# Attention and an MLP on one core: the first-layer products of half of d_ff as seven block products for eight

## The chip, the cores and the metric

The kernel runs on one core of a Trainium2 chip. The metric is the device time of one execution in microseconds, lower is better. The core has five engines with a queue each, which work in order and wait for one another by semaphores: TensorE (PE in the profile, its weight loads PEld), VectorE (DVE), ScalarE (ACT), GpSimd (POOL) and SyncE (SP), which issues most DMAs. TensorE's results go to PSUM, eight banks of 512 fp32 values for each of 128 partitions; the other data lie in SBUF.

## The reference

```python
q_n = q / (norm(q) + 1e-6);  k_n = k / (norm(k) + 1e-6)      # (8, 12, 448, 64) each
attn = softmax(q_n @ k_n.T / tau)                            # tau 0.1
x = (attn @ v).transpose(0, 2, 1, 3).reshape(3584, 768)
h = x @ w_in                                                 # 768 x 2048
g = h * clip(h + 3, 0, 6) / 6
out = g @ w_out                                              # 2048 x 768, fp32
```

## The kernel before

The eight batches of 448 tokens are worked on by pairs of heads, 48 pairs in all, six to a batch. A start-up written out by hand (`PLAN`) takes pairs 0 to 17. Then the loop of L999 runs one **turn** for each pair i from 18 to 47, some 7.8 us long, and after it a list `units[NP]` ends the work. Everything is issued in the order of the program text; no planner moves anything, so what an engine does next is what stands next in its queue.

A turn computes scores of its pair (seven 448-column matmuls in four groups, the last one, "M", apart), their exponentials on ACT (`exps`, L440), the products with v of the pair before (`values`, L462), and on DVE the division by the row sums (`finish_values`, L482 and L483: one reciprocal a pair, by which turns are found in the trace). Between them it runs **units** of the MLP, out of the list `units[i]`:

- `mm1_unit` (L561) is one of the 16 blocks of 128 columns of d_ff of one batch: six matmuls of 448 columns into one PSUM bank (L567), a relu on ACT (L576) and a product on DVE (L582) into g. Batch b's blocks run in turns 6(b+1) to 6(b+1)+5, and two are carried to the next batch's first turn.
- `product_unit` (L721) is one of the seven block products with which two blocks of 128 tokens of the second layer are computed already: eight matmuls of 384 columns (L740). It draws on sums of g that DVE makes (`g_sum`, L718), which stand in the dictionary `side` and are issued in a turn just behind `finish_values`.
- `single_unit` (L811) and `mm2_unit` (L607) are the second layer's other products.

Behind each unit `whole_units` (L940) issues its work on ACT and on DVE. In a turn the order is: scores of three groups, their six exponentials, values, `finish_values`, the sums of `side`, the first unit, the scores M and their exponential, the other units with the odd turns' norms and copies between them, the row sums of squares of a later pair (`reduce`, L238), loads of later q, k and v (`LQ`, `LV`, on SP), and the first group of values.

PSUM banks of scores and units come out of one ring of six (`next_bank`, L163); a bank is written again when its readers are done. Raw q and k lie in seven buffers (five from pair 26 on), their squares in two, values in three, all parts of the tile `big`, whose unused end also holds g of the last batch and late sums (`tail`, L531). The probabilities (`at`) go round six buffers.

Of the kernel before, what the change touches and what calls it, by code (L numbers as in the profile page):

```python
# [61 lines left out]
def kernel(  # L62
# [43 lines left out]
    gs = {x: const.tile([128, KC, 128], BF16, name=f"gs{x}", tag=f"gs{x}") for x in ("1", "6", "70", "71")}  # L106
    KM = 3 * 128
    kz = [const.tile([128, 4 * 128], BF16, name=f"kz{i}", tag=f"kz{i}") for i in range(2)]
    km = const.tile([128, 2, 128], BF16, name="km", tag="km")
# [25 lines left out]
    def raw_before(j):  # L135

        return j - NR if j < 26 else j - NR + 2

    def raw_buffer(j):
        return raws[j % NR if j < 26 else (j - 26) % (NR - 2)]  # L140

# [15 lines left out]
    ring_n = [0]  # L157

    def next_bank():
        ring_n[0] += 1  # L160
        return ring[(ring_n[0] - 1) % len(ring)]

    raw_of, sq_of, nrm_of, at_of, on_of = {}, {}, {}, {}, {}  # L163
# [37 lines left out]
    def load_v(d):  # L201
        needs(("VC", 2 * (d - NV)), ("VC", 2 * (d - NV) + 1))
        b, n = 2 * d // HP, 2 * d % HP
        for g in range(2):
            f = v[b, HP * g + n : HP * g + n + 2].rearrange("i (p c) d -> p i (c d)", c=7)
            t = vr[d % NV][:, 2 * g : 2 * g + 2, :, :].rearrange("p i c d -> p i (c d)")
            for half in range(2):
                o = t[64 * half : 64 * half + 64, :, (1 - half) * D : (5 - half) * D]
                nc.sync.dma_start(out=o, in_=f[:, :, 3 * half * D : (3 * half + 4) * D])

    def square(j, e, c0, n):

        heads = range(c0 // 7, (c0 + n - 1) // 7 + 1) if j < 2 else (0, 1)
        needs(("RE", j - 2), *(("LQ", j, g) for g in heads))
        if j not in sq_of:
            sq_of[j] = sqs[j % 2], []
        sq, have = sq_of[j]
        have.extend(range(c0, c0 + n))
        if j < 2:
            o, i = (x[:, :, :, :].rearrange("p g c d -> p (g c) d")[:, c0 : c0 + n, :] for x in (sq, raw_of[j]))  # L220
        else:
            o, i = sq[:, :, c0 : c0 + n, :], raw_of[j][:, :, c0 : c0 + n, :]
        if e == "a":
            nc.scalar.activation(out=o, in_=i, func=AF.Square)  # L224
        else:
            engines[e].tensor_tensor(out=o, in0=i, in1=i, op=ALU.mult)  # L226
# [58 lines left out]
    def vcast(i, e):  # L285
        needs(("LV", i // 2), ("VA", i - NVX, 3))
        t = vr[i // 2 % NV][:, i % 2, 1:5, :]
        f = bass.AP(tensor=t.tensor, offset=t.offset, ap=[t.ap[0], [9 * D, 2], [D, 4], [1, D]])
        o = vx[i % NVX][:, :, 0:D].rearrange("p (g c) d -> p g c d", g=2)
        if e == "v":  # L290
            nc.vector.tensor_reduce(out=o, in_=f.rearrange("p g c (d x) -> p g c d x", x=1), axis=AX.X, op=ALU.max)
            return
        (engines[e].copy if e == "a" else engines[e].tensor_copy)(out=o, in_=f)  # L293
# [101 lines left out]
    def scores(i, g, bank=None):  # L395
# [9 lines left out]
        for n, name in enumerate(GROUPS[g]):  # L405
            if name == "M":
                rows, c0 = slice(0, 128), KM
            else:
                rows = slice(64 * n, 64 * n + 64)
                c0 = 128 * int(name[1])  # L410
            if bank is None:
                o, key = bank_of(None, 1)
                keys.append(key)
                o = o[:, 0:S]
            else:
                o = SC[bank][:, n, 0:S]
            if name == "M" and i < HP:
                for rows in (slice(0, 64), slice(64, 128)):
                    nc.tensor.matmul(o[rows, :], kt[rows, KM : KM + SR], qt[rows, :], start=True, stop=True)
            else:  # L420
                ks = km[:, i % 2, :] if name == "M" and i >= XJ else kt[rows, c0 : c0 + 128]
                nc.tensor.matmul(o, ks, qt[rows], start=True, stop=True)  # L422
            out.append(o)
        sc_of[(i, g)] = (out if bank is None else [SC[bank][:, 0 : len(GROUPS[g]), 0:S]]), keys
        if g == 3:
            issued.add(("SM", i))

    def exps(i, g):
        m = len(GROUPS[g])
        at = ats[m][at_n[m] % len(ats[m])]  # L430
        at_n[m] += 1
# [98 lines left out]

    def tail(c, n):  # L531

        assert 2 * RAW <= c and c + n <= (NR + 2) * RAW + NV * VAL
        return big[:, c : c + n]

    TAIL = 2 * RAW
    g_last = tail(TAIL, FCN * (S + SR) // 2).bitcast(BF16).rearrange("p (f n) -> p f n", f=FCN)
    TAIL += FCN * (S + SR) // 2

# [21 lines left out]
    def mm1_unit(b, fc):  # L561
        needs(*(("CX", i) for i in range(b * HP, (b + 1) * HP)))
        assert len(weights) <= 6 - 2 * (2 * fc // FCN)
        x, g, c0 = xT[b % 2], g_of(b), b % 2 * SR
        ps, key = bank_of(None, 1)
        for cc in range(CC):
            nc.tensor.matmul(  # L567
# [13 lines left out]
        def product(u):  # L581
# [8 lines left out]
            unread[key] = 0  # L590
            g_done.add((b, fc))

        post["a"].append(relu)
# [44 lines left out]
    def second(b):  # L638
# [12 lines left out]
    banks, parts, ready = {}, {}, set()  # L651
    late_sums = [
        {x: tail(c, SUM).bitcast(BF16).rearrange("p (c n) -> p c n", c=KC) for x, c in zip("167e", range(c, c + 4 * SUM, SUM))}
        for c in (TAIL, TAIL + 3 * SUM)
    ]
    late_sums[0].pop("e")
    TAIL += 7 * SUM
    wide = [big[:, c : c + MH] for c in range(0, 3 * MH, MH)]
    wide_late = [tail(c, MH) for c in range(TAIL, TAIL + 2 * (len(PAIRS) - LOOP) * MH, MH)]

# [59 lines left out]

    def product_unit(n, name, end=None, apart=False):  # L721

# [4 lines left out]
        base = None if apart else {"2": "4", "5": "3", "6": "1"}.get(name)  # L727
        if base is None:
            banks[n, name] = bank_of(None, 1)
        ps, key = banks.pop((n, base)) if base else banks[n, name]  # L730
        c0, width = (MH // 2 * end, MH // 2) if end in (0, 1) else (0, MH)
# [6 lines left out]
        m = ps[:, c0 : c0 + width]  # L738
        for c in range(KC):
            nc.tensor.matmul(  # L740
# [5 lines left out]
                skip_group_check=True,  # L746
            )
        issued_products.add((n, name))
        d, e = d_and_e(n)
# [61 lines left out]
    def single_unit(b, m):  # L811

        t = 2 + b % 2
        assert all((x, c) in summed for x in ("y3", "y4") for c in range(KC)) and (b, "e") in g_summed
        ps, key = bank_of(None, 1)
        w = w_out_sb[:, :, m * MH : m * MH + MH].rearrange("p (c k) m -> p c k m", k=2)
        for n in range(2):
# [24 lines left out]
    def products(text):  # L842
# [26 lines left out]
        43: sums(6, "75"), 44: sums(6, "62"), 45: sums(6, "1"), 46: sums(7, "75"), 47: sums(7, "62"),  # L869
    }  # L870
    units = {}
    carry = firsts(1, FCN - 2, FCN - 1)
    for b in range(2, B - 1):
        first = firsts(b, *range(FCN))
        for n, x in enumerate([0, 3, 3, 3, 3, 2]):
            i = (b + 1) * HP + n
            u = carry + [first.pop(0) for _ in range(x)]
            carry = []
            *p, last = products(TURNS[i])
            if i == NP - 1:  # L880
                p, last = [last], None
# [6 lines left out]
    b = B - 1  # L888
    f = firsts(b, *range(FCN))
    units[NP] = sums(7, "1") + carry[:1] + products("4.7") + carry[1:] + [(g_left, B - 2)] + products("2.7")  # L890
    units[NP] += products("3.8") + sums(8, "75") + products("1.7 4.8") + sums(8, "62") + products("6.7 5.8") + sums(8, "1")
    units[NP] += products("7.7") + sums(B - 2, "e")
    for n, x in enumerate("2176"):
        units[NP] += f[n : n + 1] + products(x + ".8")
    units[NP] += f[4:] + products(f"s{B - 2}.0") + sums(9, "75") + products(f"s{B - 2}.1") + sums(9, "62")
    units[NP] += products("3.9 4.9") + sums(9, "1") + products("5.9") + sums(10, "75") + products("2.9 3.10") + sums(10, "62")
# [43 lines left out]
    def whole_units(n, engines="av"):  # L940
        for _ in range(n):
            unit()
            for e in engines:
                while post[e]:
                    finish_units(e)

    OPS = {
# [48 lines left out]

    if FIRST + 6 < NP:
        do("LQ", FIRST + 6)
    for i in range(FIRST, NP):  # L999
# [39 lines left out]
        if not even:  # L1039
            prepare(("NO", (i + 3) // 2))  # L1040
            if n_u > 3 and stream[0][0] is product_unit and units[i][1][0] is mm1_unit:
                do("UU", 1)
                n += 1
            prepare(("CK", i + 1), ("CK", i + 2))
# [4 lines left out]
        do("UU", 1)  # L1049
        prepare(("RE", i + 5), ("LQ", i + 7))  # L1050
        if not even:
            prepare(("LV", (i + 5) // 2))
        while post["p"]:
# [44 lines left out]
```

## Time and profile before

| what | value |
|---|---|
| runs | 405.30, 405.31, 406.76 us; median 405.31 us |
| profiled execution | 404.91 us, its span 403.1 us |
| granted TensorE clock | 1.000 |
| DVE busy | 286.4 us, 71% of the span, 503 instructions |
| ACT busy | 278.3 us, 69% |
| POOL busy | 234.0 us, 58% |
| first-layer matmuls (L567) | 768 of 448 columns |
| second-layer block products (L740) | 624 matmuls, 608 of them of 384 columns, 16 of 192 |

A span runs from the first to the last instruction; the rest of an execution's time lies around it. A matmul's duration on the page runs to a modelled end and overlaps the next one, so the rate at which TensorE works is read from the starts of matmuls that follow one another: the chain of waits lists them so.

### The profile page before, as it was taken

To read this page: it belongs to the slowest core of one execution; us is meant where nothing else is said; L and a number is where in the kernel's file an instruction comes from. 1 tells how busy PE (TensorE), PEld (TensorE's weight loads), DVE (VectorE), ACT (ScalarE), POOL (GpSimd) and SP (SyncE) were. 2 spreads that over 40 slices of the span, in tenths; PEclk is the share of its full clock that TensorE was granted. 3 is DMA by queue.
4 is the path that set the end of the run, shared out by engine and by line. 5 is a ranking of instruction groups with operands and counts; after the bars stand their busy time and mean duration, and the time that the engine had idled before them with its cause. 6 is when DMAs were issued, how large, how long until landed. Compare 5 with 4: busy or idle time off the path is not lost.

```text
span 403.1 us, 9619 instructions
## 1 busy us (share of the span) xinstructions
PE 395.5 (98%) x3696; PEld 234.3 (58%) x3696; DVE 286.4 (71%) x503; ACT 278.3 (69%) x609; POOL 234.0 (58%) x228
## 2 busy tenths in 40 slices
PE   7999999999999999999999999999999999999996
PEld 4666656555655556556555556555565556555563
DVE  5898768766998777776867888687656566644663
ACT  5999998798467686786858768668658755225230
POOL 7799655662384997488386865766665500510070
PEclk9999999999999999999999999999999999999999
DMA  8999989979988659786989659976963523130134
GB/s 289 281 254 257 216 247 230 156 125 230 187 213 220 139 128 228 171 222 130 180 216 212 152 130 164 182 192 145 192 154 76 112 46 67 41 79 21 26 73 99
DMA packets 91566, 65.32 MB, mean 162 GB/s; under 512 B 56064, under 2 KB 89984, under 8 KB 91520
## 3 DMA queue, kind: packets, MB, share of 16 engines
q1 hardware_dynamic: 87408, 58.02, 62.8%
q0 software_dynamic: 3712, 6.29, 9.0%
q8 instruction: 29, 0.48, 0.5%
q10 hardware_dynamic: 400, 0.39, 0.3%
q14 instruction: 17, 0.14, 0.1%
HBM read 47.19 MB, written 11.01 MB: 144 GB/s over the span
## 4 chain that ended last, share of the span: by engine, by line
PE 94%; DVE 3%; DMA 1%; ACT 0%; issue 0%; DVEq 0%; ACTq 0%
PE M L567 24%; PE M L740 17%; PE PV L462 13%; PE Y L567 6%; PE M L422 6%; PE Z L567 5%; PE Y L740 4%; PE Z L740 4%; PE M L614 3%; PE M L820 2%; PE Z L422 2%; PE PV L922 2%; PE Z L820 1%; PE Y L422 1%; DVE n L238 1%; PE SC L422 1%
## 5 line engine op out<-in xcount | busy, mean ns | idle before, releaser
L440 ACT ACTIVATE at<-M 128x448 bf16<-128x448 f32 x200 | 99.9, 568 | 16.4 <-PE M L422 14.4
L567 PE MATMUL M<-xT,w_in_sb 128*128 128x448 bf16 x522 | 110.8, 352 | 0.0
L567 PEld LDWEIGHTS <-w_in_sb 128*128 128x128 bf16 x768 | 72.0, 98 | 62.6 <-issue 2.8
L274 POOL TENSOR_TENSOR nrm<-big,r 128x896 bf16<-128x896 f32 (+1 forms) x48 | 79.5, 1662 | 26.1 <-ACT r L262 19.3
L576 ACT ACTIVATE u<-M,bias 128x448 bf16<-128x448 f32 x87 | 57.0, 655 | 25.2 <-PE M L567 24.8
L582 DVE SCALAR_TENSOR_TENSOR gT<-u,M 128x448 bf16<-128x448 bf16 x76 | 46.7, 618 | 36.8 <-ACT u L576 36.3
L226 POOL TENSOR_TENSOR big<-big 128x896 f32<-128x896 f32 (+3 forms) x39 | 63.9, 1641 | 10.9 <-DMA big<-in_k_dram 5.7
L462 PEld LDWEIGHTS <-at 128*128 128x128 bf16 (+1 forms) x1536 | 54.9, 97 | 22.8 <-issue 13.5
L462 PE MATMUL PV<-vx,at 128*128 128x65 bf16 (+1 forms) x1536 | 64.3, 194 | 0.2 <-DVE on L483 0.2
L238 DVE TENSOR_REDUCE n<-big 128x14 f32<-128x896 f32 (+1 forms) x50 | 51.7, 1041 | 5.6 <-ACT big L224 4.6
L379 POOL COPY km<-tT 64x128 bf16<-64x128 bf16 x34 | 12.8, 376 | 58.1 <-DMA tT<-nrm 45.1
L769 POOL TENSOR_TENSOR big<-big 128x384 f32<-128x384 f32 x11 | 11.8, 1076 | 54.6 <-ACT big L788 54.5
L740 PEld LDWEIGHTS <-gT 128*128 128x128 bf16 x288 | 27.8, 98 | 20.0 <-DVE gT L718 0.6
L740 PE MATMUL M<-w_out_sb,gT 128*128 128x384 bf16 x208 | 37.9, 326 | 0.1
L440 ACT ACTIVATE at<-Z 128x448 bf16<-128x448 f32 x49 | 27.7, 565 | 9.9 <-PE M L422 7.3
L483 DVE TENSOR_TENSOR on<-PV,rc 128x512 bf16<-128x512 f32 x48 | 33.2, 691 | 1.7
L293 POOL CAST vx<-big 128x512 bf16<-128x512 f32 x44 | 33.2, 757 | 1.2 <-DMA big<-in_v_dram 1.1
L422 PE MATMUL M<-tT,kz 64*128 64x448 bf16 (+1 forms) x175 | 31.6, 351 | 0.0
L740 PEld LDWEIGHTS <-gs 128*128 128x128 bf16 x224 | 21.5, 98 | 14.8 <-DVE gs L718 0.4
L567 PE MATMUL Y<-xT,w_in_sb 128*128 128x448 bf16 x132 | 28.6, 352 | 0.0
L440 ACT ACTIVATE at<-Y 128x448 bf16<-128x448 f32 x45 | 25.7, 570 | 3.1 <-PE Z L422 1.7
L740 PE MATMUL M<-w_sum,gs 128*128 128x384 bf16 x144 | 26.3, 326 | 0.0
(130 smaller groups left out, 561.7 us busy)
## 6 DMA issues: line engine op xcount, KB each, us to landing
big<-in_v_dram SPq DMA_DIRECT2D x96, 128.0 KB, 4.4
big<-in_k_dram SPq DMA_DIRECT2D x24, 448.0 KB, 4.9
big<-in_q_dram SPq DMA_DIRECT2D x24, 448.0 KB, 4.4
out_dram<-o SPq DMA_DIRECT2D x107, 96.0 KB, 2.2
w_in_sb<-in_moe_w_in_dram POOLq DMA_DIRECT2D x4, 768.0 KB, 10.2
w_out_sb<-in_moe_w_out_dram POOLq DMA_DIRECT2D x4, 768.0 KB, 9.2
tT<-nrm SPq DMA_TRANSPOSE x34, 3.3
xT<-on SPq DMA_TRANSPOSE x25, 3.8
```

The source lines that it names most:

```text
L226: engines[e].tensor_tensor(out=o, in0=i, in1=i, op=ALU.mult)
L238: nc.vector.tensor_reduce(out=n2s[d % 2][:, j % 2, c], in_=sq[:, :, :, :].rearrange("p g c d -> p (g c) d")[:, c, :], axis=AX.X, op=ALU.add,)
L274: engines[e].tensor_tensor(out=nrm[:, :, g, :].rearrange("p c g d -> p g c d"), in0=raw_of[j][:, g, :, :], in1=rs[d % 2][3][:, j % 2, :] . ...
L293: (engines[e].copy if e == "a" else engines[e].tensor_copy)(out=o, in_=f)
L422: nc.tensor.matmul(o, ks, qt[rows], start=True, stop=True)
L440: nc.scalar.activation(out=o, in_=x, func=AF.Exp, scale=inv_tau)
L462: nc.tensor.matmul(pv_out(j, h), at[rows, n, q_cols(i // HP, j)], vt[rows, 3 + h if name == "M" else 5 * h + int(name[1]), :], start=(name ...
L483: nc.vector.tensor_tensor(out=on[:, :, :, :].rearrange("p j h d -> p h j d"), in0=pv4[:, :, :, 0:D], in1=rc[:, :, :].to_broadcast([128, 2, ...
L567: nc.tensor.matmul(ps[:, 0:S], w_in_sb[:, cc, fc * 128 : (fc + 1) * 128], x[:, cc, 0:S], start=(cc == 0), stop=(cc == CC - 1),)
L576: nc.scalar.activation(out=u[:, :], in_=ps[:, 0:S], func=AF.Relu, bias=half_bias, scale=1.0 / 6.0)
L582: nc.vector.scalar_tensor_tensor(out=g[:, fc, c0 : c0 + S], in0=u[:, :], scalar=1.0, in1=ps[:, 0:S], op0=ALU.min, op1=ALU.mult,)
L740: nc.tensor.matmul(m, lhs[:, c, :], rhs[:, c, c0 : c0 + width], start=(base is None and c == 0), stop=(c == KC - 1), skip_group_check=True,)
```

## The change

In batches 3 to 7, the first eight of the 16 blocks of d_ff are no longer eight `mm1_unit`s but four pairs p = 0 to 3. For a pair, the weights (256 columns of d_ff, two halves k of d_model) and the tokens (two halves j of 224) form blocks of 2 x 2, and seven products of three matmuls of 224 columns each take the place of eight. Each pair is three units, `f_a`, `f_b` and `f_c`, with other units between them. Their products are summed in two banks, x and y: y is kept out of the ring ahead of its first use (`keep_bank`). Between the parts, ACT copies a half bank to SBUF and DVE writes a sum or a difference back into PSUM, on which the next matmuls accumulate. Sums of weights are made once (`w_in_sum`: five for each p), sums of x five for each batch (`x_in_sum`, at the end of the batch's first turn). Batch 2 and the other eight blocks stay as they were.

In turns 6(b+1)+1 to 6(b+1)+4 two of three `mm1_unit`s go and one pair comes. The turn's last unit, a `product_unit`, is cut in two (`cut`): its first five matmuls (four, where only one product unit is there) stand between `f_b` and `f_c`, the rest behind `f_c`. What stands between `f_a` and `f_b` is a whole `product_unit`, in a batch's second turn an `mm1_unit`, and in turn 28 the four matmuls of the cut.

To make room, raw q and k have four buffers from pair 26 on for five, squares one from pair 24 on for two, values two from load 12 on for three (a load is of two pairs of heads), and `at` five after turn 18. Loads of q and k are issued one turn later (`LQ` of i + 6 in place of i + 7), and so are loads of values.

```diff
+    def f_a(b, p):
+        x, kx = bank_of(None, 1)
+        y, ky = keep_bank()
+        first_products(b, p, x, ("3", 0, True), ("4", 1, False))
+        d = f_copy(x[:, 0:HS])                                   # ACT, 224 columns
+        if width_of[ky] < S:
+            nc.tensor.matmul(y[:, MH:S], ident[:, :], ident[:, 0 : S - MH], start=False, ...)
+        nc.vector.tensor_tensor(out=y[:, HS:S], in0=x[:, HS:S], in1=d, op=ALU.add)
...
+    def f_b(b, p):
+        first_products(b, p, y, ("1", 1, False))
+        w = f_copy(y[:, HS:S])
+        first_products(b, p, x, ("5", 0, False), ("2", 1, False))
+        nc.vector.tensor_tensor(out=y[:, 0:S]..., in0=w (twice), in1=x[:, 0:S]..., op=ALU.subtract)
+        u = f_relu(x)
+        held.append(lambda: f_product(b, p, u, x, kx, 1))
...
+    def f_c(b, p):
+        first_products(b, p, y, ("7", 0, False), ("6", 1, False))
+        # then relu of y on ACT and the product of y on DVE
...
+    side_late = {HP * (b + 1): [(x_in_sum, b, "34167")] for b in range(3, B - 1)}
+    for n, (i, x, e) in enumerate(((23, "62751", "v"), (24, "62751", "p"), (25, "62751", "v"), (26, "62751", "v"))):
+        side_late[i] = [(w_in_sum, n, x, e)] + side_late.get(i, [])
...
+                if not p:
+                    l0, l1 = cut(last, 4)
+                    units[i] = u + [ua, l0, ub, l1, uc]
+                else:
+                    l0, l1 = cut(last)
+                    p += u
+                    if n > 1:
+                        p.reverse()
+                    units[i] = [p[0], ua, p[1], ub, l0, uc, l1]
...
+    fill = products("2.8 1.8 7.8 6.8") + f
+    for x in sevens:
+        units[NP] += [x[0], fill.pop(0), x[1], fill.pop(0), x[2]]
...
-        prepare(("RE", i + 5), ("LQ", i + 7))
-        if not even:
-            prepare(("LV", (i + 5) // 2))
+        prepare(("RE", i + 5))
+        for f, *args in side_late.get(i, []):
+            f(*args)
+        if i <= FIRST:
+            do("LQ", i + 7)
+        elif i > FIRST + 1:
+            prepare(("LQ", i + 6))
+        if even and i > FIRST:
+            prepare(("LV", (i + 4) // 2))
```

## The prediction

> **What bounds the kernel now.** First the engines and the chain that ended last, from the page:
>
> ```profile
> PE 395.5 (98%) x3696; PEld 234.3 (58%) x3696; DVE 286.4 (71%) x503; ACT 278.3 (69%) x609; POOL 234.0 (58%) x228
> PE 94%; DVE 3%; DMA 1%; ACT 0%; issue 0%; DVEq 0%; ACTq 0%
> ```
>
> TensorE is the bound: it holds 94% of the chain, and DVE's 3% lies mostly in the start-up. So matmul columns taken out are worth their full time, as long as no other engine gets onto the chain. The chain of waits in order of time shows the rate of matmuls, and the one place in the loop where DVE did get onto it (start us, us, what):
>
> ```profile
> 219.72 0.61 PE PV L462 x16
> ...
> 221.29 1.92 DVE gs L718
> 223.21 0.02 issue
> 223.23 2.07 DVE gT L718
> 225.30 0.05 issue
> 225.35 1.48 PE M L740 x8
> ```
>
> ```profile
> 395.92 1.95 PE M L740 x12
> 397.87 0.66 PE Y L740 x8
> ```
>
> Twelve matmuls of 384 columns take 1.95 us, 162.5 ns each; eight of 192 take 0.66, 82.5 each. That is a fixed 2.5 ns and 0.417 ns a column. At 221 to 225 two sums of g, 0.68 us as a rule, took 2 us, the product unit that reads them stood, and TensorE lost 0.3 us. VectorE, at 71% on average, is thus already close to the edge where a unit waits on its sums.
>
> Next, how a turn looks to each queue. Turn 31, the second turn of batch 4's first layer, begins with its scores at 211.17 (the reciprocal L482 of pair 30 at 212.53 is its `finish_values`). In the timeline VectorE, then TensorE:
>
> ```profile
> 211.37 1.08 DVE L238 TENSOR_REDUCE n<-big 128x14 f32<-128x896 f32 x1
> 212.53 0.21 DVE L482 RECIPROCAL rc<-PV 128x8 f32<-128x8 f32 x1
> 212.77 0.69 DVE L483 TENSOR_TENSOR on<-PV,rc 128x512 bf16<-128x512 f32 x1
> 213.38 0.68 DVE L718 TENSOR_TENSOR gs<-gT 128x1024 bf16<-128x1024 bf16 x1
> 214.10 0.69 DVE L718 TENSOR_TENSOR gT<-gT 128x1024 bf16<-128x1024 bf16 x1
> ```
>
> ```profile
> 212.33 1.46 PE L740 MATMUL M<-w_out_sb,gT 128*128 128x384 bf16 x8
> 213.63 0.35 PE L422 MATMUL M<-tT,km 128*128 128x448 bf16 x1
> 213.82 2.43 PE L567 MATMUL M<-xT,w_in_sb 128*128 128x448 bf16 x12
> ```
>
> VectorE goes from one instruction to the next without idle time until 214.79; only later it idles. Turn 32 begins at 219.00; ScalarE there:
>
> ```profile
> 221.51 0.59 ACT L440 ACTIVATE at<-Z 128x448 bf16<-128x448 f32 x1
> 221.94 0.69 ACT L576 ACTIVATE u<-M,bias 128x448 bf16<-128x448 f32 x1
> 222.45 0.61 ACT L440 ACTIVATE at<-M 128x448 bf16<-128x448 f32 x1
> 222.88 0.70 ACT L576 ACTIVATE u<-M,bias 128x448 bf16<-128x448 f32 x1
> ```
>
> Six exponentials hold it until 221.94, the first unit's relu and the exponential of M until 222.88. Anything issued behind these waits for that time.
>
> **What is taken out.** A pair had 12 matmuls of 448 columns: 12 x 2.27 / 12 (the chain gives 2.27 us for 12) = 2.27 us. Its seven products are 21 of 224 columns, each 2.5 + 224 x 0.417 = 95.8 ns: 2.01 us. Saved 0.26 us a pair, for 20 pairs **-5.2 us**. The weight loads double, yet 16 matmuls of 65 columns in `values`, each with its own load, take 0.47 us in the chain, so loads hide. The identity matmul of 64 columns, at 0.03 us by that row, comes at most once a pair: between 0 and 0.6, taken **+0.3**.
>
> **What is added: links from TensorE over ScalarE and VectorE back to TensorE.** Durations by the nearest rows: d or w, a copy of 224 columns on ScalarE, 0.37 (L224 has 0.31 for 128 and 0.40 for 256 columns, L759 0.48 for 384). The addition of f_a 0.39 (L765: 0.36 for 192, 0.56 for 384 columns), the subtraction of f_b, 448 columns, 0.62. A sum of x, 672 bf16 values, 0.50, and a sum of weights, 384, 0.35 (L718: 0.68 for 1024; L689: 0.94 for 1536, so 0.52 ns a value). VectorE to TensorE 0.05 (the issue line at 225.30).
>
> *A batch's second turn.* The five sums of x are issued at the end of the first turn, behind `reduce` L238. In turn 31 that ends at 212.45; five by 0.50 end at 214.95. Queued behind them: L482 and L483 (0.85), the two sums L718 (1.41), then the addition of f_a, all in order: 214.95 + 0.85 + 1.41 + 0.39 + 0.05 = 217.65. TensorE would be at f_b at: 213.82 + f_a 0.575 + `mm1_unit` 1.135 = 215.53. It waits 2.1 us. In turn 25 and 43 the same three steps follow; in turn 37 a copy L558 of 0.42 and an L765 of 0.56 stand in place of L718's 1.41, and it waits 1.8. Together **+8.1**. Bounds: 0.44 a sum (back to back, less 0.06) gives 7; with each sum stopped as at 221, over 15. I take the unhindered one, since GpSimd idles from 211.6 to 215.5 in this trace. In turn 25 it doesn't: five sums of weights are put on it just before.
>
> *The other twelve turns.* Turn 32: f_a would end at 222.05 and the unit behind it, 1.30, at 223.35. ScalarE reaches d at 222.88 and ends at 223.25; VectorE has by then the first unit's product (222.66 to 223.28). Addition to 223.70, TensorE at 223.75: a wait of 0.4, twelve times **+4.8**. In turn 28 only four matmuls (0.65 for 1.30) cover it: **+0.65**. Bounds: 0 if ScalarE came 0.4 sooner; and 0.27 more for each sum L718 ahead of the addition, its mean of 0.95 against 0.68, for 18 such sums 4.9 in all.
>
> *The second link.* Behind f_b's last matmul x drains (0.16, a matmul's 352 ns on the page less its 189), the subtraction takes 0.62, links 0.09: 0.87. It is covered by five matmuls, 0.81; in turn 28 by four, 0.65. With VectorE free **+1.2** for the 16 in the loop; bounds 0 and 0.3 each, 4.8.
>
> *Sums of weights.* Those at the ends of turns 25 and 26 take VectorE 5 x 0.35 = 1.75 each, ahead of the next turn's L482, which had 0.65 idle before it at 176.94: 1.1 each on a chain that already waits, **+2.2** (0 to 3.5). Those in turn 23 hit a turn without a pair: 0, hidden by the 7.8 us until the first f_a.
>
> *After the loop.* VectorE and ScalarE are half idle, a cover is 1.30 or 1.13 us, against 0.16 + 0.04 + 0.37 + 0.03 + 0.39 + 0.05 = 1.04 for the first link: 0, at most 1.5 if the sums of x (2.5 us of VectorE at 349) make "1.8" late.
>
> *Fewer buffers.* Loads of q and k come one turn later. They land 4.9 us after issue (page), and the square in a turn begins 2 to 5 us after the scores. GpSimd would wait up to 2.9 us for some, and it has idle time in most turns: 0, at most 3. The one square buffer waits for L238 of the pair before, at the turn's beginning: 0, hidden by the same idle time. Five `at` buffers: the third group's is then last read at the previous turn's end: 0.
>
> **Sum**: -5.2 + 0.3 + 8.1 + 4.8 + 0.65 + 1.2 + 2.2 = +12.05. The profiled execution took 404.91 us (span 403.1), 0.4 under the median of the runs: **417 us**. TensorE has no idle time elsewhere in the loop in which such waits could be made good.
>
> **Rivals.** (1) *Faster: the links end under their covers.* Then only -5.2 + 0.3 + about 0.6 of the second link is left: 400.6 us. For it: ScalarE and VectorE have 30% idle, and the addition misses its cover in twelve turns by 0.4 only. Against it: in a second turn the addition would have to end 2.1 us earlier, and the program puts five sums, a division and two sums in front of it, with no idle time between. It decides from the point where the addition of f_a ends within 1.1 to 1.3 us of f_a's end in most turns.
>
> (2) *GpSimd stops the sums.* In turn 32 GpSimd squared and normalised while L718 ran:
>
> ```profile
> 220.96 1.68 POOL L226 TENSOR_TENSOR big<-big 128x896 f32<-128x896 f32 x1
> 222.60 2.14 POOL L274 TENSOR_TENSOR nrm<-big,r 128x896 bf16<-128x896 f32 x1
> ```
>
> The first sum, 1.99 long, ends about 0.6 after L226 does; the second likewise after L274. If five sums of x, not two sums, meet this, a good half of them lose 1 us each. As a sum: 4.9 for L718 ahead of additions, 3 more in turn 25 against GpSimd's sums of weights, 1 to 2 among the rest: 417 + 9 = 426. Against it: GpSimd was idle where three of four sets of sums fall. [...]
>
> (3) *Late loads.* GpSimd, 7.9 of 8.0 us busy from 219 to 227, falls a turn behind, and the copies km, scores M and TensorE with it: 1 us in some eight turns on top, 425.
>
> **Numbers.** My forecast 0.59, rival 1 0.16, rival 2 0.19, rival 3 0.06. My forecast's own range is 411 to 425, from its lower bounds (8.1 to 7, 4.8 to 2, the second link at 0) to its upper ones short of rival 2. The range that takes in most of the others is 403 to 427: outside lie most of rival 1 and a part of rival 2. About 0.5%, 2 us, is what a measurement can tell from no change. Faster by more, under 403.3: 0.16, rival 1. Within: 0.06, rival 1 with a wait left, or my forecast with half of each. Slower: 0.78.
>
> **What would show it.** In the profile after: PE's busy share falls and a group of PE idle or DVE pieces appears on the chain, at the first matmul of the "1" product, behind the addition; some 2 us in each of turns 25, 31, 37, 43, and 0.4 in the others. The starts of 224-column matmuls should be 96 ns apart; 110 would cost 6 us more. L482 of the second turn should come 2.5 us later after its scores. If the chain stays on TensorE at 94% and the addition's end lies ahead of the cover's, I am wrong, and rival 1 holds. Sums of x of over 1 us each show rival 2; scores M that wait for km show rival 3.

## The result and the profile after

The changed kernel takes 452.77 us, the median of five runs (452.06 to 456.10); before, on the same chip, 405.31 us (404.72 to 406.76). The ratio is 1.1186, 95% interval 1.113 to 1.1241: slower by 47 us, where 12 were forecast. The profiled execution took 452.38 us, its span 450.6 us.

The page of the kernel after: TensorE's and the other engines' busy time, the granted clock in 40 slices, and the chain by engine.

```profile
PE 409.1 (91%) x3878; PEld 255.2 (57%) x3878; DVE 324.9 (72%) x583; ACT 291.8 (65%) x649; POOL 240.1 (53%) x233
PEclk9999999999999998969999999899999799999999
PE 59%; DVE 17%; DMA 9%; POOL 5%; SPq 4%; issue 3%; ACT 3%; POOLq 0%; DVEq 0%; ACTq 0%
```

The span grew by 47.5 us. TensorE's idle time (span less busy) went from 403.1 - 395.5 = 7.6 to 41.5 us, which is 33.9 of them. The other 13.6 are busy time, although 5 us of columns were taken out. Part of them is the clock: its row, all nines before, has an 8, a 6, an 8 and a 7, and with a mean of 0.977 it can have taken at most 450.6 x 0.023 = 10 us. The rest of the busy time is not parted here. TensorE holds 59% of the chain for 94%; DVE, DMA, POOL and the queue of SP have the rest.

Turn 32 is the turn whose VectorE, ScalarE and GpSimd lines the prediction was worked out from. In the kernel after it begins some 24 us later. Its timeline, VectorE first (start us, us, operation, in brackets the idle time ahead of it and who ended it):

```profile
245.31 0.69 DVE L505 TENSOR_TENSOR on<-PV,rc 128x512 bf16<-128x512 f32 x1
245.92 1.52 DVE L882 TENSOR_TENSOR gs<-gT 128x1024 bf16<-128x1024 bf16 x1
247.47 2.05 DVE L882 TENSOR_TENSOR gT<-gT 128x1024 bf16<-128x1024 bf16 x1
249.45 0.61 DVE L617 SCALAR_TENSOR_TENSOR gT<-u,M 128x448 bf16<-128x448 bf16 x1
249.98 0.39 DVE L711 TENSOR_TENSOR Y<-M,u 128x224 f32<-128x224 f32 x1
```

GpSimd, ScalarE and TensorE in the same turn:

```profile
245.90 0.99 POOL L957 TENSOR_TENSOR o<-o,big 128x384 f32<-128x384 f32 x1
246.85 2.12 POOL L247 TENSOR_TENSOR big<-big 128x896 f32<-128x896 f32 x1
248.94 2.13 POOL L295 TENSOR_TENSOR nrm<-big,r 128x896 bf16<-128x896 f32 x1
```

```profile
247.32 0.42 ACT L696 COPY u<-M 128x224 f32<-128x224 f32 x1
```

```profile
246.77 1.46 PE L914 MATMUL M<-w_out_sb,gT 128*128 128x384 bf16 x8
250.42 0.45 PE L685 MATMUL Y<-big 128*128 128x224 bf16 x3 [2.19 <-DVE Y L711]
```

The copy d (L696) ends at 247.74, inside its cover, the product unit of 246.77, as the prediction had it. The addition (L711) could have come then; it starts at 249.98, because the two sums of g ahead of it took 3.6 us for 1.4. The first began beside GpSimd's L957 and ended at 247.44, 0.55 us after it; the second, beside L247, at 249.52, 0.55 after that one. In turn 31 of the same trace, with GpSimd idle, the two take 0.68 and 0.69 us. TensorE waited 2.19 us where 0.4 was forecast.

The late loads show in the waits of the kernel after (who waited for what: us in total, times, the longest); before, the first line stood at 5.7 us and the third at 0.8:

```profile
POOL big L247 <- DMA big<-in_k_dram: 34.7, 11, 4.9
POOL big L247 <- DMA big<-in_q_dram: 24.5, 10, 5.3
DVE n L259 <- POOL big L247: 17.2, 10, 3.7
```

### The profile page after: what moved, and what is told of

Same layout as the page of the kernel before. It is cut to its first block, busy times and chain, and to the rows that moved or that the text cites. A ratio compares the mean times of both kernels' runs of the same rounds, so it can differ in the third digit from the quotient of the medians.

```text
span 450.6 us, 10185 instructions
## 1 busy us (share of the span) xinstructions
PE 409.1 (91%) x3878; PEld 255.2 (57%) x3878; DVE 324.9 (72%) x583; ACT 291.8 (65%) x649; POOL 240.1 (53%) x233
## 4 chain that ended last, share of the span: by engine, by line
PE 59%; DVE 17%; DMA 9%; POOL 5%; SPq 4%; issue 3%; ACT 3%; POOLq 0%; DVEq 0%; ACTq 0%
PE M L602 10%; PE M L914 9%; PE PV L484 8%; PE M L685 5%; DMA big<-in_q_dram 5%; PE M L443 3%; DVE big L672 3%; PE Y L914 3%; DMA big<-in_k_dram 3%; PE Y L602 3%; PE Z L602 3%; POOL big L247 2%; PE M L780 2%; DVE gs L882 2%; DVE n L259 2%
## 5 line engine op out<-in xcount | busy, mean ns | idle before, releaser
L247 POOL TENSOR_TENSOR big<-big 128x896 f32<-128x896 f32 (+3 forms) x39 | 64.0, 1642 | 70.5 <-DMA big<-in_k_dram 34.7
L295 POOL TENSOR_TENSOR nrm<-big,r 128x896 bf16<-128x896 f32 (+1 forms) x48 | 79.4, 1657 | 23.7 <-ACT r L283 17.6
L602 PE MATMUL M<-xT,w_in_sb 128*128 128x448 bf16 x336 | 72.4, 352 | 0.4 <-DMA xT<-on 0.4
L484 PEld LDWEIGHTS <-at 128*128 128x128 bf16 (+1 forms) x1536 | 55.9, 98 | 27.5 <-issue 18.7
L602 PEld LDWEIGHTS <-w_in_sb 128*128 128x128 bf16 x528 | 48.5, 98 | 40.3 <-issue 3.1
L259 DVE TENSOR_REDUCE n<-big 128x14 f32<-128x896 f32 (+1 forms) x50 | 52.0, 1043 | 22.3 <-POOL big L247 17.2
L484 PE MATMUL PV<-vx,at 128*128 128x65 bf16 (+1 forms) x1536 | 65.3, 195 | 2.1 <-DVE on L505 2.1
L617 DVE SCALAR_TENSOR_TENSOR gT<-u,M 128x448 bf16<-128x448 bf16 x51 | 31.4, 617 | 13.0 <-ACT u L611 12.5
L914 PE MATMUL M<-w_out_sb,gT 128*128 128x384 bf16 x208 | 40.3, 334 | 0.0
L914 PEld LDWEIGHTS <-gT 128*128 128x128 bf16 x288 | 28.9, 102 | 17.4 <-issue 2.4
L443 PE MATMUL M<-tT,kz 64*128 64x448 bf16 (+1 forms) x175 | 34.5, 355 | 2.8 <-DVE o L941 2.2
L505 DVE TENSOR_TENSOR on<-PV,rc 128x512 bf16<-128x512 f32 x48 | 33.2, 691 | 1.7
L914 PE MATMUL M<-w_sum,gs 128*128 128x384 bf16 x144 | 28.1, 334 | 5.2 <-DVE big L973 3.9
L685 PEld LDWEIGHTS <-big 128*128 128x128 bf16 x150 | 15.2, 102 | 30.5 <-issue 27.4
```

Source lines behind the costliest of these rows:

```text
L259: nc.vector.tensor_reduce(out=n2s[d % 2][:, j % 2, c], in_=sq[:, :, :, :].rearrange("p g c d -> p (g c) d")[:, c, :], axis=AX.X, op=ALU.add,)
L295: engines[e].tensor_tensor(out=nrm[:, :, g, :].rearrange("p c g d -> p g c d"), in0=raw_of[j][:, g, :, :], in1=rs[d % 2][3][:, j % 2, :] . ...
L484: nc.tensor.matmul(pv_out(j, h), at[rows, n, q_cols(i // HP, j)], vt[rows, 3 + h if name == "M" else 5 * h + int(name[1]), :], start=(name ...
L505: nc.vector.tensor_tensor(out=on[:, :, :, :].rearrange("p j h d -> p h j d"), in0=pv4[:, :, :, 0:D], in1=rc[:, :, :].to_broadcast([128, 2, ...
L602: nc.tensor.matmul(ps[:, 0:S], w_in_sb[:, cc, fc * 128 : (fc + 1) * 128], x[:, cc, 0:S], start=(cc == 0), stop=(cc == CC - 1),)
L685: nc.tensor.matmul(bank[:, j * HS : (j + 1) * HS], lhs[:, c, :], rhs[:, c, :], start=start and c == 0, stop=c == 2, skip_group_check=True,)
```

## The experiments

Each experiment compares with the kernel before on the same chip, where that took 405.7 to 407.2 us.

**Parts of the change undone, one at a time.** The buffers and later loads alone, without the seven products:

```diff
+    side_late = {}
...
-            sevens = b > 2 and 1 <= n <= NF
+            sevens = False
...
-    f = firsts(b, *range(2 * NF, FCN))
+    f = firsts(b, *range(FCN))
```

> All products of the first layer as before the change, with the changed kernel's fewer raw, square, value and at buffers and its later loads. Theory L (q and k land late, the square on GpSimd and with it the row sums of squares on VectorE come late, and everything behind them in VectorE's queue): 418 us or more. Theory S (the sums and links of the seven products fill VectorE's queue): 405 to 408 us. The prediction on record, which put the buffers at nothing: 405 us.

Measured 423.03 us, ratio 1.0382 (1.028 to 1.0484): a part that the prediction put at 0 to 3 us costs 16. The timeline of its turn 32, SP's queue, GpSimd and VectorE:

```profile
226.37 0.58 SPq L217 DMA_DIRECT2D big<-in_k_dram  x1
...
230.42 1.68 POOL L247 TENSOR_TENSOR big<-big 128x896 f32<-128x896 f32 x1 [4.65 <-DMA big<-in_k_dram]
...
232.14 1.09 DVE L259 TENSOR_REDUCE n<-big 128x14 f32<-128x896 f32 x1 [4.40 <-POOL big L247]
...
233.14 0.20 DVE L504 RECIPROCAL rc<-PV 128x8 f32<-128x8 f32 x1
```

The load is issued at 226.37; GpSimd, which has been idle for 4.65 us, can square it at 230.42; VectorE stands at its reduction for 4.40 us, since it takes its work in order, and the reciprocal, the sums of g and the units' products stand behind it. GpSimd had the idle time that the prediction counted on; VectorE did not.

The sums left out, then the links left out (`no_sums` multiplies raw blocks; `no_links` has no copies, addition and subtraction):

```diff
-            engines[e].tensor_tensor(out=first_sum[x, p] if o is None else o, in0=y, in1=z, op=op)
-            engines[e].tensor_tensor(out=x_sum[x], in0=y, in1=z, op=op)
```

> The changed kernel without the sums of weights and of x: the products read raw blocks, so what is left out is those additions alone. Theory S: 405 to 412 us, as 25 us or more of VectorE's work ahead of the additions is gone. Theory L: 425 to 440 us, since GpSimd's waits for DMA, 59 us in the changed kernel, stay. The prediction on record: 417 less 8.1 and 2.2 and with 0.4 in the four second turns: 408 us.

```diff
-        d = f_copy(x[:, 0:HS])
-        nc.vector.tensor_tensor(out=y[:, HS:S], in0=x[:, HS:S], in1=d, op=ALU.add)
-        w = f_copy(y[:, HS:S])
-        nc.vector.tensor_tensor(out=y[:, 0:S]..., in0=w (twice), in1=x[:, 0:S]..., op=ALU.subtract)
```

> The changed kernel without the two copies, the addition and the subtraction by which ScalarE and VectorE hand a pair's partial sums on, so TensorE waits for neither inside a pair. Left out: these four instructions of each pair. Theory S with links as its main part: 410 us or less. Theory L: 430 us or more, as late sums of x still hold the products. The prediction on record: 400 to 405 us.

Measured 433.66 us without the sums (ratio 1.0643, 1.0545 to 1.0741) and 439.85 us without the links (1.0795, 1.0686 to 1.0904). Taking out either leaves most of the loss.

The whole change with the loads back at the turn's beginning (the buffers' numbers stay as changed):

```diff
+        if i > FIRST + 1:
+            prepare(("LQ", i + 6))                 # behind finish_values and the sums of side, ahead of the first unit
...
-        elif i > FIRST + 1:
-            prepare(("LQ", i + 6))                 # at the turn's end
```

> The changed kernel with the load of q or k for i + 6 issued at the beginning of turn i, ahead of the first unit, not at its end. Theory L: GpSimd's waits for DMA fall from 59 us to under 20 and the time to 420 to 432 us. Theory S: 447 us or more, no change to speak of.

Measured 449.13 us, ratio 1.1023 (1.0869 to 1.1177): only 3.6 us less than the changed kernel by the medians, 6.6 by the ratios, and the two intervals overlap. What costs 16 us by itself costs far less when all is there.

**What about the loads.** Kernel before with one square buffer; kernel before with loads of q and k one turn later; the first experiment with early loads:

```diff
-        needs(("RE", j - 2), *(("LQ", j, g) for g in heads))           # one_square
+        needs(("RE", j - 2 if j < 25 else j - 1), *(("LQ", j, g) for g in heads))
...
-            sq_of[j] = sqs[j % 2], []
+            sq_of[j] = sqs[j % 2 if j < 24 else 0], []
```

> The kernel before with one buffer for squares from pair 24 on in place of two, nothing else. By it a square on GpSimd waits for the row sums of squares of the pair before on VectorE, which waits for its own square. Theory Q (the single square buffer ties the two engines to one another and is the main part of the 16 us of the buffers): 412 us or more. Theory D (the later loads are): 405 to 408 us.

```diff
-        prepare(("RE", i + 5), ("LQ", i + 7))
+        prepare(("RE", i + 5))                     # later_loads
+        if i <= FIRST:
+            do("LQ", i + 7)
+        elif i > FIRST + 1:
+            prepare(("LQ", i + 6))
```

> The kernel before with q and k loaded one turn later, all buffers as before. Theory D (the square waits for its data and the row sums on VectorE with it): 412 us or more, and GpSimd waits for DMA of q and k over 30 us. Theory Q: 405 to 408 us, with at most 20 us of such waits.

> The kernel without seven products and with the fewer buffers, q and k loaded at the beginning of a turn, not at its end. Theory D: 405 to 410 us, for the data are there when the square's turn comes. Theory Q: 415 us or more, as the single square buffer stays.

Measured: one square buffer 406.42 us (1.0005, 0.9974 to 1.0036), later loads 418.01 us (1.0292, 1.0191 to 1.0393), all buffers fewer with early loads 405.56 us (0.9981, 0.9957 to 1.0004). The number of buffers costs nothing. The time of issue costs 12 us by itself; that it makes all of the 16 is not shown to the microsecond, but the two intervals overlap, and with early loads nothing is left. The waits of `later_loads`:

```profile
POOL big L226 <- DMA big<-in_k_dram: 46.9, 12, 5.9
DVE n L238 <- POOL big L226: 36.3, 15, 4.6
```

VectorE's wait for the square went from 0.8 to 36.3 us.

**Sums and links again, on kernels whose loads are repaired.** First both left out with the late loads, then with early ones, then one of them each:

> The changed kernel without the sums of weights and x, and without the copies, addition and subtraction between products: the seven products, the fewer buffers and the later loads are left. If the three causes add up (buffers and loads 16, sums 19, links 13, columns saved 5): 416 to 420 us, that is the run with buffers and loads alone less 3 to 7. If the products of 224 columns cost more than 96 ns each, or the parts hide one another: 423 us or more.

> The changed kernel with q and k loaded at the beginning of a turn, without the sums of weights and x and without the copies, addition and subtraction between products. If the columns saved are real and late loads were all that was left: 400 to 403 us. If the second kept bank or the order of units costs by itself (score matmuls that wait for bank y): 404 to 412 us.

> The same with the copies, addition and subtraction in place, still without the sums of weights and x. Links by the prediction on record (0.4 a pair in the loop for the first, under 0.3 for the second): 7 to 9 us over the run without either. If links are worth more since VectorE's row sums, sums of g and products stand ahead of them: 12 us or more over it.

> The same with the sums of weights and x in place and without the copies, addition and subtraction. Sums by the prediction on record (2.1 us in each second turn, 2.2 in batch 3): about 10 us over the run without either. If GpSimd and VectorE, tied by the one square buffer and by the sums that read SBUF from both sides, hold one another up: 18 us or more over it.

| kernel | us | ratio, 95% interval |
|---|---|---|
| `no_sums_no_links` (late loads) | 427.93 | 1.0536, 1.0449 to 1.0623 |
| `early_no_sums_no_links` | 408.53 | 1.0058, 1.0032 to 1.0084 |
| `early_no_sums` (links kept) | 426.49 | 1.0487, 1.0434 to 1.0539 |
| `early_no_links` (sums kept) | 425.86 | 1.0471, 1.0419 to 1.0523 |

The links cost 426.49 - 408.53 = 18.0 us and the sums 17.3; the walk of the prediction has about 8 (4.8 + 0.65 + 1.2 and four second turns' 0.4) and about 9 (8.1 less those, and 2.2). Both twice as much. And the bare products, three matmuls for four, don't gain: 408.53 is 3 us above `loads_alone_early`. The waits of TensorE in `early_no_sums_no_links`, of which the kernel before has none:

```profile
PE M L443 <- DVE o L930: 2.2, 4, 0.6
PE M L903 <- DVE gT L871: 0.9, 2, 0.5
PE M L903 <- DVE gs L871: 0.4, 1, 0.4
PE M L443 <- DVE gT L718: 0.4, 1, 0.4
```

Scores wait for a bank that VectorE has yet to read, and a cut product unit, which now comes sooner in its turn, waits for its sums: 3.9 us in all. The starts of 224-column matmuls are 96 ns apart, so the columns are saved. The waits take more than the saving back, since one among the scores also breaks up matmuls that would have started together (Y and Z at 235.83): of 155 score matmuls of 64 rows that follow another behind 105 us, 92 start within 0.06 us of it in the kernel before and 82 here. Counted from start to start in the two traces, the scores lose 6.6 us and the rest 1.7; less 5.2 of columns that is the 3 us.

**The change after the loop only** (seven products in batch 7 alone, old buffers and loads, sums of weights at the ends of turns 45 to 47):

> Seven products in batch 7 alone, after the loop, where VectorE and ScalarE are half idle; all buffers and loads as in the kernel before; sums of weights on GpSimd and VectorE in turns 45 to 47. By the prediction's walk (links end under covers of 1.1 to 1.3 us there, 0.26 us a pair saved): 404.0 to 405.0 us, about 0.2% under the kernel before. If the waits seen in the changed kernel there (0.8 us twice) stay: 405 to 407 us.

Measured 406.72 us, the median of twelve runs, ratio 1.0005 (0.9986 to 1.0024): nothing. The waits view has 1.3 us, in two waits of TensorE, for the addition, against 4 x 0.26 = 1.0 us of columns.

**Does the place of the sums ahead of the addition cost the links so much?** The sums of g issued behind `f_a`'s addition instead; then, in the whole kernel, that and the sums of x and weights spread out:

```diff
         nc.vector.tensor_tensor(out=y[:, HS:S], in0=x[:, HS:S], in1=d, op=ALU.add)
+        issue_behind()                             # in f_a
...
-        for f, *args in side.get(i, []):
-            f(*args)
+        behind.extend(side.get(i, []))
+        if not any(x[0] is f_a for x in stream):
+            issue_behind()
```

> As the run with early loads and without sums of weights and x, with one step moved: in turns with a pair the sums of g are issued on VectorE behind the addition of f_a, not ahead of it. If the links cost 18 us since the addition stands behind sums of g that GpSimd holds up: 412 to 418 us, and no wait of TensorE over 1 us at the products behind the addition. If the links' own length (copy, addition, subtraction, queue of exponentials) is the cost: 423 us or more.

```diff
+        if p == 0 and 2 < b < B - 1:
+            x_in_sum(b, "1")                       # behind the addition
...
+        if p == 0 and 2 < b < B - 1:
+            x_in_sum(b, "67")                      # behind the subtraction
...
+    side_late = {HP * (b + 1): [(x_in_sum, b, "34")] for b in range(3, B - 1)}
+    for n, (i, x, e) in enumerate(((20, "62751", "v"), (21, "62751", "v"), (22, "62751", "v"), (23, "62751", "v"))):
```

> The changed kernel, whole, with q and k loaded at the beginning of a turn, the sums of g behind the addition of f_a, the sums of weights in turns 20 to 23, and the sums of x split: two at the end of a batch's first turn, one behind the addition, two behind the subtraction. If the place in VectorE's queue makes the loss: 415 to 425 us, where the same work in the old places took 449. If VectorE's load by itself, or GpSimd's hold on it, makes the loss: 435 us or more.

Both came out slower than the same work in the old places (426.49 and 449.13): 441.66 us (1.088, 1.0841 to 1.092) and 462.22 us (1.1387, 1.1347 to 1.1426). The theory fell. VectorE and TensorE in turn 31 of `early_no_sums_behind`:

```profile
225.62 1.32 DVE L888 TENSOR_TENSOR gs<-gT 128x1024 bf16<-128x1024 bf16 x1
226.98 2.06 DVE L888 TENSOR_TENSOR gT<-gT 128x1024 bf16<-128x1024 bf16 x1
```

```profile
229.09 0.99 PE L920 MATMUL Z<-w_out_sb,gT 128*128 128x384 bf16 x5 [2.30 <-DVE gT L888]
```

The addition now comes within 0.3 us of its time. But the two sums, 0.68 and 0.78 us in this turn of `early_no_sums`, have moved beside GpSimd's L247 and L295 (224.72 to 228.49), and the product unit waits for them. It isn't their place in VectorE's queue, it is their length.

**GpSimd's large operations left out**, for later pairs, in `early_no_sums` and in `loads_early`:

```diff
+        if j > 22:                                 # square
+            return
...
+        if j <= 20:                                # normalise
             engines[e].tensor_tensor(...)
```

> As the run with early loads and without sums of weights and x, and GpSimd's squares and products with the norms left out from turn 18 on, so that GpSimd holds nothing that VectorE's sums of g need. If the links cost 18 us since those sums take 2 us beside GpSimd: 413 to 418 us (the prediction's walk gives 8 us of links over 408.5), sums of g at 0.7 us, and the granted clock at 1.000. If the links' own length is the cost: 422 us or more.

> The changed kernel with early loads and all its sums, with GpSimd's squares and products with the norms left out from turn 18 on. If GpSimd's hold on sums is what makes links and sums cost twice what the prediction walked out: 420 to 428 us, against 449 with GpSimd's work. If VectorE's own load makes the loss: 438 us or more.

Measured 415.76 us (1.0236, 1.0163 to 1.0309) for links alone and 424.40 us (1.0449, 1.0387 to 1.0511) for links and sums. Turn 32 of `early_no_gp`, VectorE and TensorE:

```profile
232.06 0.68 DVE L884 TENSOR_TENSOR gs<-gT 128x1024 bf16<-128x1024 bf16 x1
232.77 0.69 DVE L884 TENSOR_TENSOR gT<-gT 128x1024 bf16<-128x1024 bf16 x1
...
233.91 0.39 DVE L713 TENSOR_TENSOR Y<-M,u 128x224 f32<-128x224 f32 x1
```

```profile
234.36 0.45 PE L687 MATMUL Y<-big 128*128 128x224 bf16 x3
```

The same sums take 0.68 and 0.69, the addition ends at 234.30, and `f_b` comes 0.15 us late behind the unit before it, where the prediction had 0.4. Without GpSimd's operations the links cost 415.76 - 408.53 = 7.2 us and the sums 424.40 - 415.76 = 8.6, the walk's sizes. One reservation: the 408.53 still has GpSimd at work. Leaving its operations out also takes away VectorE's waits for them, but those are small: the waits view has VectorE 1.0 us behind squares in `loads_early`, 2.6 us behind GpSimd in all, and in `early_no_sums` none behind squares. What changes is the length of the sums: the 29 sums of g in turns 25 to 46 take 32.1 us in `loads_early` and 21.1 in `early_no_gp`, the 20 sums of x in the loop 13.0 and 10.0. TensorE's waits at the addition follow, first in `loads_early`, then in `early_no_gp`:

```profile
PE Z L685 <- DVE Z L711: 10.2, 2, 5.4
PE M L685 <- DVE M L711: 10.2, 8, 2.2
PE Y L685 <- DVE Y L711: 6.2, 2, 4.1
```

```profile
PE M L687 <- DVE M L713: 4.5, 5, 1.7
PE Z L687 <- DVE Z L713: 3.4, 2, 1.8
PE Y L687 <- DVE Y L713: 1.7, 1, 1.7
```

That is 26.6 us against 9.6.

## Why the prediction was right and wrong

**Right**: the direction; that TensorE saves 0.26 us a pair (96 ns a matmul); that the links miss their covers and put VectorE on the chain, at the first matmul of the "1" product behind the addition; that fewer buffers cost nothing. Where little disturbs a turn its walk holds: in turn 31, with GpSimd idle from 236.8 on, the addition keeps TensorE for 2.34 us, forecast 2.1, and the reciprocal of pair 30 comes 3.3 us later behind the scores than before (232.81 to 237.48, against 211.17 to 212.53), forecast 2.5; the difference is in the five sums of x, 3.25 us for 2.5. In `early_no_gp` the four second turns lose 1.85, 1.8, 1.3 and 1.8 us at the addition, counted from start to start, where 2.1, 2.1, 1.8 and 2.1 were forecast, and most other turns 0.15 to 0.25 for 0.4.

**Wrong**: the size, 47 us for 12. The medians of the runs give a ladder from the kernel before to the kernel after:

| step | us | forecast |
|---|---|---|
| fewer buffers, early loads (`loads_alone_early`) | +0.3 | 0 |
| products cut to seven (`early_no_sums_no_links`) | +3.0 | -4.9 |
| links, GpSimd's large operations left out | +7.2 | about 8 |
| sums, likewise | +8.6 | about 9 |
| GpSimd's large operations back (`loads_early`) | +24.7 | 0 |
| loads at the turn's end (the changed kernel) | +3.6 | 0, at most 3 |

The rows were measured on different chips, on which the kernel before took 405.3 to 407.2 us. By the ratios to it the last two steps are 23 and 7 us, the others within about 1 us of the table.

*The step that failed most* is "I take the unhindered one, since GpSimd idles from 211.6 to 215.5 in this trace", and the same choice for the sums L718 ahead of the additions and for the sums of weights at 0.35 us. The durations were right for VectorE without GpSimd's large operations beside it: in `early_no_gp` a sum of x takes 0.50 us on average and the two sums of g in turn 32 0.68 and 0.69; the shortest sum of weights in the kernel after takes 0.35. The addition itself kept its 0.39 us in all 16 pairs of the loop. But the prediction took GpSimd's idle time from the old turn, and once TensorE waits, the turn is longer and GpSimd's work lies elsewhere in it: in turn 31 of `loads_early` the two sums of g took 2.05 and 2.06 us beside L247 and L295, and TensorE waited 4.1. Turn 25 and the start of turn 26 of the kernel after on VectorE:

```profile
174.26 4.89 DVE L672 TENSOR_TENSOR big<-xT 128x672 bf16<-128x672 bf16 x5
...
187.66 1.72 DVE L658 TENSOR_TENSOR w_in_sb<-w_in_sb 128x384 bf16<-128x384 bf16 x1
189.30 1.84 DVE L658 TENSOR_TENSOR big<-w_in_sb 128x384 bf16<-128x384 bf16 x1
```

Five sums of x took 4.89 us for 2.5 beside GpSimd's sums of weights (L658, 175.35 to 180.78), and two sums of weights 3.6 for 0.7 beside L247 and L295. So 3.4 and 5.5 us of TensorE were lost in turns 25 and 26 (its starts stop from 178.83 to 182.42 and from 190.25 to 195.95), where 2.1 and 0.4 + 1.1 were in the sum. Rival 2 named this lengthening beside GpSimd and put it at 9 us; in the ladder it is 25, with the slower clock that comes with it (0.973 in `loads_early`, 0.999 in `early_no_gp`). Its cause inside the chip is not shown; the lengths are.

The rival, too, was mis-sized by its count: it had 18 sums of g at their old mean of 0.95 us and some of the sums of x. That allows 0.27 us a sum; the stretched pair in turn 32 cost TensorE 1.8 us more than the walk has.

In the kernel after itself TensorE's waits at the additions come to 20.5 us in the waits view (8.6, 7.4 and 4.5), against 15.75 in the sum (8.1 + 4.8 + 0.65 + 2.2). So these terms, too small as they were, miss only some 5 of the 35 us. Waits that were no term of the sum are beside them, among them 3.9 us for L973, which adds up second-layer products, 2.2 for banks of scores (L941), 2.1 for the division L505, 1.3 for sums of g and 1.2 for sums of x; and the clock took up to 10.

*"Fewer buffers ... 0, at most 3".* The price by itself was 12 to 16 us. The prediction looked for the wait on the engine that does it, found idle time there, and stopped. The one that pays is VectorE, at `reduce` L238, in order ahead of everything that the next turn needs. In the whole kernel the same loads cost 3.6 us by the medians. A reason can be read from the traces: with late loads VectorE waits 17.2 us for squares, 1.0 with early ones, but the squares then meet the sums of g less, and the 29 of turns 25 to 46 take 25.7 us, 32.1 with early loads. Rival 3 had a like mechanism at 8 us, but through the copies km: in `later_loads` those wait no longer than before (15.2 us for tT after 45.1), and the reduction is what is late.

*"TensorE has no idle time elsewhere"* was taken to mean that nothing else could be lost. The waits for banks and sums, which come from the units' new order alone, were no term of the sum: 3.9 us as idle time, 8.3 from start to start with the scores that no longer start together. Less the 5.2 us saved they make the 3.0 of this step.

*After the loop*, "at most 1.5", TensorE lost 0.82 and 0.78, as a gap between starts at 414.98 and 400.65: just over the upper end, and it eats the saving of batch 7 (`tail_only`).

No kernel tried beats the one before; fewer buffers with early loads equals it. Not tried, and so open: to move GpSimd's large operations to where VectorE has no sums, and to keep TensorE busy during the waits.

## What to carry to other kernels

An operation on a chain that leaves the bounding engine and comes back to it is priced at the length it has beside the neighbour's work, not at its length alone (here a sum of g: 0.68 us with GpSimd idle, up to 2.06 beside its L247 and L295): after the change the turns are longer, and what was idle beside it need not be. Idle time of the engine that waits for a later load was no cover here (in `loads_alone` GpSimd sat idle for 4.65 us and VectorE behind it for 4.40); follow on to the engine that reads its result in order, and see what is queued behind that wait. And when units change places for fewer columns, walk the waits of the new order first: five microseconds of columns went in waits of half a microsecond.

## What the runs showed of the hardware

**The granted clock fell after some of the waits.** In the kernel after, behind the wait that ended at 195.95, the windows (busy us and instructions of PE, PEld, DVE, ACT and POOL, then the granted clock, DMA share and GB/s):

```profile
186.00:195.00 9.00, 4.47 (x43) 2.69 (x40) 8.86 (x12) 4.47 (x11) 7.63 (x7) 0.96 0.10 23
195.00:200.00 5.00, 4.05 (x19) 2.76 (x19) 2.14 (x5) 0.98 (x2) 0.00 (x0) 0.50 0.68 144
200.00:204.00 4.00, 4.00 (x51) 2.53 (x50) 2.66 (x6) 3.11 (x7) 1.00 (x1) 0.87 0.20 44
```

The same form at half and at full rate, TensorE in that turn:

```profile
196.46 1.33 PE L685 MATMUL M<-xT,w_in_sb 128*128 128x224 bf16 x6
...
204.10 0.74 PE L685 MATMUL M<-big,w_in_sb 128*128 128x224 bf16 x6
```

Waits of 5.5, 4.2 and 3.65 us (turns 26, 43, 36) were followed by half rate, and so were one of 2.0 us (turn 24, ended at 171.41) and in `early_no_sums` one of 2.2 us (230.34 to 232.74). Those of 2.35 and 2.5 us (turns 32, 31) and one of 3.4 us (turn 25) were not. In the kernel after, the slow stretches behind these waits last 3.41 us or twice that: 173.7 to 177.2 in turn 24, 194.2 to 201.0 in turn 26, 286.4 to 289.8 in turn 36, 347.8 to 354.7 in turn 43. The length of the wait alone does not part the two kinds: 2.0 us was enough, and 3.4 not. Nor does TensorE's busy share in as long a stretch. In the 3.41 us just before the drop TensorE was busy for 39% in `early_no_sums` (229.9 to 233.4) and for 59% in turn 24 (170.3 to 173.7). The wait of turn 25 lay in two stretches of that length, 177.1 to 180.5 and 180.5 to 183.9, busy for 60% and 45%: 59% was followed by half rate and 45% was not. What decides is not shown. The mean clock was 0.977 in the kernel after, 0.973 in `loads_early`, and 0.999 in `early_no_gp`. Of the 27.0 us between the spans of the last two (449.4 and 422.4), 7.2 are TensorE's busy time (407.6 and 400.4), and 449.4 x 0.027 = 12 us is the most that the clock can have taken: that much at most was paid a second time, at TensorE, for VectorE's longer sums.

**GpSimd's operations were longer beside the sums, not always.** In turn 32 its L247 took 2.12 us beside the sums, against its mean of 1.70, and the norms L295 began behind it, at 248.94. In the kernel before, L226 took 2.20 us beside the sum that began at 177.79, and 1.68 beside the one at 221.21.
